# First attention rebuilt by tiles: a three-stage block on one Trainium2 core

## The chip, the cores and the metric

One kernel, launched once, on one core of a Trainium2 chip. Its time is the device time of an execution in microseconds; a time is given as the median of several executions. The core has TensorE (matmuls, weight loads), VectorE, ScalarE, GpSimd, and SyncE, whose queue issues every DMA here. Everything is float32 to the outside.

## The reference

Three blocks follow one another, for 4 images (B) of 576 positions (S). The second block's output is the third's input.

```python
# 1: attention, 8 heads of 64, causal window of 128, distance bias
scores = q @ k.T / 8 + slopes[h] * -abs(rel)      # kept where 0 <= rel < 128
attn = exp(scores - max); attn /= sum + 1e-9
x = (attn @ v)                                    # heads side by side: 512 features
# 2: gated block
h = relu(x @ w_in); u, v = h[:512], h[512:]       # 512 features each
v_n = (v - mean) / sqrt(var + 1e-6)
x = (u * (w_spatial @ v_n + b_spatial)) @ w_out
# 3: four experts of 64 features, top 2 of 4 by x @ w_gate
for e in range(4):
    a = softmax(causal(x @ wq[e] @ (x @ wk[e]).T / 8))
    out += gate[e] * (a @ (x @ wv[e]) @ wo[e])
```

w_in and w_out arrive as 64-bit floats, as integer words, and are turned into float32 on the core.

## The kernel before

**Two kinds of matmul.** Where operands are plain float32, a matmul is two instructions on TensorE. The dense products are done otherwise: an operand is split into a high part (a cast to the reduced form fp32r) and a low part (what is left, `lo_part`, L123), and three products of parts are added up (PASSES, L34). A split costs a cast on ScalarE (or GpSimd) and a subtraction on VectorE for every operand.

**First attention** (L330 to L476, loop L608 to L643). Positions go in five tiles per image, four of 128 and one of 64 (j = 4). The loop has 80 steps (image, tile, pair of heads). Step s does, in this order: `normalise` of step s-1; `scores` of step s (matmuls into one buffer of a PSUM bank, a masked copy that folds the window's two blocks into 128 columns, then for each head a VectorE instruction that adds the bias and takes the row's extreme, and a ScalarE exponential that sums its row: `row_softmax`, L187); some ticks of weight decode; half of the step's dense work; `transposes` of step s-2 (two per step, a ScalarE copy, two GpSimd selects that separate the window's blocks again); the other half; after each tile's fourth step `attend` of the tile three steps back, whose two heads go to two column halves of the array, and whose result is split into x.

For image 0 the score operands are raw float32 on 64 rows, one head at a time. For images 1 to 3 they are split: `load_chunk` (L332) brings K and Q of a tile twice, into both halves of the partitions, and `split_chunk` (L350) makes of K one operand with high part above and low part below (KK), of Q a high and a low copy (qh, ql). Two matmuls of 128 rows then give a head's scores.

**Dense work** is a list of generators (`Dense`, L37) that the loop pulls from by a budget in nominal nanoseconds: 1200 per step up to step 20, then 1650. Per image it holds `v_tile` (5 tiles, 512 columns), `u_half` (2 halves of 4 groups of 12 matmuls, 288 columns) and `spatial` (8 groups of 14). A piece is taken when its x tiles and its weights are there in the order of the program. Each group accumulates in one of three PSUM buffers (psD, L110). `spatial` multiplies by u, splits the result into high and low part and stores both to DRAM (g_dram, L119, L573 to L582).

**Weights.** `in_weights` (L225) decodes w_in in eight pieces on ScalarE, VectorE and GpSimd; the loop advances it by three ticks a step for six steps, then by five (L618). `setup` (L295) prepares the spatial weights, and w_out through DRAM.

**Order.** TensorE's order is that of the program text (L1033). The other engines and SyncE's queue are ordered by a planner at build time, which takes work as it becomes ready by its own estimates.

**Second stage and second attention** (L650 to the end). w_out is folded into the projection weights (`fold`, L678, pw). For each image `load_g` (L702) reads both parts of the gated result; `proj` (L759) makes q, k (pq) and v with gates (pvB). Its `spread` copies the split q and k by DMA into both halves of the partitions, 24 transfers an image, so that `scores_b` (L829) takes two matmuls of 128 rows for each head; tile 4 uses four per half of the columns. PSUM holds three single buffers for scores and two for dense groups (psD). The loop L934 has 40 steps and runs the projection of the next image as dense work.

Of the kernel before, what the change touches and what calls it, by code (L numbers as in the profile page):

```python
# [100 lines left out]
def block_kernel(ctx, tc, qT, qTt, kT, v, w_in, wspT, bsp, w_outT, wcat, wo, rel, relt, low, tri, out):  # L101
# [7 lines left out]
    psX = psA.enter_context(tc.tile_pool(name="psX", bufs=2, space=PSUM))  # L109
    psD = psA.enter_context(tc.tile_pool(name="psD", bufs=3, space=PSUM))  # L110
# [8 lines left out]
    g_dram = dram.tile([B, 2, 4, P, S], F32, name="g_dram")  # L119
# [175 lines left out]
    def setup():  # L295
# [11 lines left out]
        def spatial_bias():  # L307

            st = d2.tile([P, S], F32, tag="f64w", name="st_bias", bufs=2)
            hi = d2.tile([P, S], F32R, tag="g0", name="bias_hi", bufs=2)  # L310
# [19 lines left out]
    raws, QL_, V_ = {}, {}, {}  # L330

    def load_chunk(b, j):  # L332

        q0, qn = TOK[j]
        rq = a1.tile([P, 1024], F32, tag="rawq" if b else "qh", name=f"rq{b}_{j}", bufs=1 if b else 2)
        own = b > 0 or j == 2
        rk = a1.tile([P, H, P], F32, tag="rawk" if own else "ql", name=f"rk{b}_{j}", bufs=1 if own else 2)
        for half in range(2 if b else 1):
            sl = slice(64 * half, 64 * half + 64)
            if j < 4:  # L340
                nc.sync.dma_start(rq[sl, :].rearrange("p (h c) -> p h c", h=H), qT[b, :, :, q0 : q0 + P])
            else:
                nc.sync.dma_start(rq[sl, :768], qTt[b])
            nc.sync.dma_start(rk[sl, :, :qn], kT[b, :, :, q0 : q0 + qn])
        vt = a1.tile([P, 512], F32, tag="v", name=f"v{b}_{j}", bufs=4)
        nc.sync.dma_start(vt[:qn], v[b, q0 : q0 + qn])
        raws[b, j] = (rq, rk)
        V_[b, j] = vt

    def split_chunk(b, j, part):  # L350
        q0, qn = TOK[j]
        rq, rk = raws[b, j]
        w = 1024 if j < 4 else 768
        kk = KK[:, :, q0 : q0 + qn]
        if part == 0:
            nc.scalar.copy(kk, rk[:, :, :qn])
            qh = a1.tile([P, 1024], F32R, tag="qh", name=f"qh{b}_{j}")
            ql = a1.tile([P, 1024], F32R, tag="ql", name=f"ql{b}_{j}")
# [10 lines left out]
    xready, now = {}, [0]  # L369
    st_ = {}  # L370

    def score_operands(b, j, hp, k0, kn):

        heads = []
        for o in range(2):
# [76 lines left out]
    def attend(i):  # L452
# [6 lines left out]
        for t, w in ((j - 1, pT[0]), (j, pT[1])):  # L459
            if t < 0:  # L460
                continue
# [575 lines left out]
```

## Time and profile before

| | us |
|---|---|
| median of 3 runs | 554.91 (551.39 to 555.55) |
| profiled execution | 556.01 |
| its span, first to last instruction | 554.2 |

| engine | busy us | share | instructions |
|---|---|---|---|
| TensorE matmuls | 500.2 | 90% | 3876 |
| TensorE weight loads | 449.2 | 81% | 3876 |
| VectorE | 340.3 | 61% | 1200 |
| ScalarE | 286.8 | 52% | 859 |
| GpSimd | 247.1 | 45% | 536 |

The mean granted TensorE clock was 0.985 of full speed. DMA moved 75.02 MB. The shares are means over stages that differ, so the stretches are to be read one by one. A matmul's duration in the trace holds its passage through the array, which the next one overlaps; how far apart matmuls start says what they cost in a row. In the rows PE is TensorE (PEld its weight loads), DVE VectorE, ACT ScalarE, POOL GpSimd, SP SyncE (SPq its queue), L405 line 405; out<-in names what an instruction writes and reads. An image's tiles are counted on: tile 5 is the first of image 1, tile 10 the first of image 2.

### The profile page before, as it was taken

The page shows a single profiled execution, that of the slowest core. Times are in us where ns is not written, and L with a number is a line of the kernel's source. Part 1 is how long each engine was busy: PE and PEld are TensorE (multiplying, and loading weights), DVE is VectorE, ACT ScalarE, POOL GpSimd, SP SyncE. Part 2 cuts the span into 40 slices and gives each one's busy share as a digit, 9 for nine tenths or more (in the row PEclk, how much of TensorE's full clock was granted, in tenths as well). Part 3 has the DMA queues.
Part 4 walks back from the last instruction along what each step waited for, and adds up shares of the span by engine and source line. Part 5 has one row for each costly group of instructions (what it writes and reads, how often), then busy time and mean ns, then how long its engine had stood idle before and what let it go on. Part 6 is the DMA issues. An engine that isn't in the chain of part 4 may idle for free.

```text
span 554.2 us, 11535 instructions
## 1 busy us (share of the span) xinstructions
PE 500.2 (90%) x3876; PEld 449.2 (81%) x3876; DVE 340.3 (61%) x1200; ACT 286.8 (52%) x859; POOL 247.1 (45%) x536
## 2 busy tenths in 40 slices
PE   4556986898999999999999999989899999999993
PEld 3444776697878899899898999979889999998882
DVE  2899868597877787687654643315463463446640
ACT  4455545475556675566543522324564554565851
POOL 3887864666774688556651000003241232232430
PEclk9999999798999999999999999999999999999997
DMA  9962246645876348621037068289755522641111
GB/s 232 262 195 78 71 117 152 169 118 157 228 188 133 80 93 186 181 73 39 2 130 256 19 238 285 56 209 257 173 190 136 139 60 71 142 117 46 39 39 58
DMA packets 68674, 75.02 MB, mean 135 GB/s; under 512 B 13638, under 2 KB 44486, under 8 KB 68616
## 3 DMA queue, kind: packets, MB, share of 16 engines
q1 hardware_dynamic: 68616, 74.29, 50.0%
q8 instruction: 31, 0.51, 0.4%
q14 instruction: 27, 0.22, 0.1%
HBM read 43.86 MB, written 16.25 MB: 108 GB/s over the span
## 4 chain that ended last, share of the span: by engine, by line
PE 67%; DMA 9%; DVE 9%; POOL 4%; ACT 4%; SPq 3%; issue 2%; DVEq 0%; POOLq 0%; ACTq 0%
PE pv L486 9%; PE pg L566 7%; PE pq L787 7%; PE pvB L808 5%; PE pxB L898 5%; PE pout L916 5%; PE pu L549 5%; DMA rk<-in_kT 5%; PE px L466 4%; PE ps L405 4%; PE psB L840 4%; PE ptB L878 4%; PE pw L686 3%; PE pt L431 2%; PE psB L849 2%
## 5 line engine op out<-in xcount | busy, mean ns | idle before, releaser
L189 ACT ACTIVATE p<-p,st 128x128 f32<-128x128 f32 x144 | 56.8, 396 | 34.0 <-DVE st L188 29.2
L196 POOL TENSOR_SCALAR p<-p,st 128x128 f32<-128x128 f32 x144 | 64.4, 457 | 15.5 <-DVE st L193 12.1
L486 PE MATMUL pv<-win,x 128*128 128x512 f32 x240 | 68.5, 420 | 0.5 <-ACT x L127 0.4
L566 PE MATMUL pg<-wsp,vn 128*128 128x288 f32 x384 | 63.4, 304 | 0.0
L549 PE MATMUL pu<-x,win 128*128 128x288 f32 x384 | 60.2, 301 | 0.0
L192 POOL TENSOR_SCALAR stB<-stB 128x2 f32<-128x2 f32 (+1 forms) x40 | 9.2, 230 | 112.7 <-ACT pB L189 107.2
L787 PE MATMUL pq<-x,W 128*128 128x288 f32 x384 | 56.4, 299 | 0.0
L566 PEld LDWEIGHTS pg<-wsp,vn 128*128 128x128 f32 x384 | 54.5, 192 | 0.0
L549 PEld LDWEIGHTS pu<-x,win 128*128 128x128 f32 x384 | 52.9, 188 | 0.5 <-issue 0.2
L787 PEld LDWEIGHTS pq<-x,W 128*128 128x128 f32 x384 | 52.1, 188 | 0.5 <-DVE hl L124 0.2
L486 PEld LDWEIGHTS pv<-win,x 128*128 128x128 f32 x240 | 44.0, 199 | 8.2 <-ACT x L127 0.9
L196 POOL TENSOR_SCALAR pB<-pB,stB 128x128 f32<-128x128 f32 (+4 forms) x72 | 39.4, 559 | 24.5 <-DVE stB L861 18.9
L189 ACT ACTIVATE pB<-pB,stB 128x128 f32<-128x128 f32 (+3 forms) x64 | 35.8, 560 | 26.8 <-DVE stB L188 24.0
L431 PE MATMUL pt<-ident,p 128*128 128x128 f32 x128 | 30.2, 308 | 18.5 <-POOL p L196 16.3
L192 POOL TENSOR_SCALAR st<-st 128x2 f32<-128x2 f32 (+1 forms) x80 | 25.7, 322 | 40.5 <-ACT p L189 36.0
L444 POOL TENSOR_SCALAR_AFFINE_SELECT pU<-pT 128x256 f32<-128x256 f32 (+1 forms) x64 | 31.6, 494 | 24.8 <-ACT pT L432 12.9
L405 PE MATMUL ps<-rk,rq 64*128 64x128 f32 (+1 forms) x144 | 29.5, 361 | 13.9 <-DMA rk<-in_kT 7.3
L431 PEld LDWEIGHTS pt<-ident,p 128*128 128x128 f32 x128 | 17.8, 147 | 28.1 <-POOL p L196 22.3
L405 PEld LDWEIGHTS ps<-rk,rq 64*128 64x128 f32 x144 | 24.8, 255 | 19.1 <-issue 7.8
L188 DVE CUSTOM_DVE_ANT_0 p<-ps,relm 128x128 f32<-128x128 f32 x128 | 31.5, 283 | 13.3 <-DMA relm<-in_rel 8.7
L188 DVE CUSTOM_DVE_ANT_0 pB<-psB,trit 128x128 f32<-128x128 f32 (+3 forms) x64 | 29.6, 487 | 13.4 <-PE psB L840 13.4
L808 PE MATMUL pvB<-W,x 128*128 128x260 f32 (+1 forms) x240 | 32.8, 286 | 4.3 <-DVE hl L124 4.3
(139 smaller groups left out, 1175.2 us busy)
## 6 DMA issues: line engine op xcount, KB each, us to landing
g_dram<-g SPq DMA_DIRECT2D x32, 288.0 KB, 3.0
q<-hl SPq DMA_DIRECT2D x64, 144.0 KB, 2.8
x<-g_dram SPq DMA_DIRECT2D x8, 1024.0 KB, 5.6
rq<-in_qT SPq DMA_DIRECT2D x28, 256.0 KB, 4.3
rk<-in_kT SPq DMA_DIRECT2D x28, 256.0 KB, 4.6
kk<-hl SPq DMA_DIRECT2D x32, 144.0 KB, 2.5
out<-ot SPq DMA_DIRECT2D x18, 256.0 KB, 2.0
v<-in_v SPq DMA_DIRECT2D x16, 256.0 KB, 3.1
```

Source lines behind the costliest of these rows:

```text
L188: nc.vector.tensor_tensor_reduce(s_view, ps_view, tab, -0.125, FLT_MAX, ALU.add, ALU.min, nm)
L189: nc.scalar.activation(s_view, s_view, AF.Exp, bias=nm, scale=-1.0, accum_out=sm)
L192: nc.gpsimd.tensor_scalar(dst, src, 1e-9, 0.0, op0=ALU.add, op1=ALU.add)
L196: nc.gpsimd.tensor_scalar(p, p, r, 0.0, op0=ALU.mult, op1=ALU.add)
L405: nc.tensor.matmul(ps[:, o, c : c + w], lhs, rhs, start=(n == 0), stop=(n == len(ops) - 1))
L431: nc.tensor.transpose(pt[:, o, :], p[:, o, :], ident)
L444: nc.gpsimd.affine_select(out=u_, in_=h, pattern=[[-i, n] for i, n in pattern], compare_op=ALU.is_gt, fill=0.0, base=0, channel_multiplier=1)
L486: nc.tensor.matmul(pv, x[i][:, k, t0 : t0 + P], win[j][:, k, 512:1024], start=(n == 0), stop=(n == 11))
L549: nc.tensor.matmul(pu[:, :HALF], win[i][:, k, m * P : (m + 1) * P], x[j][:, k, c], start=(n == 0), stop=(n == 11))
L566: nc.tensor.matmul(pg[:, :HALF], vn[i][k][:, m * P : (m + 1) * P], wsp[j][:, k, c], start=(n == 0), stop=False)
L787: nc.tensor.matmul(pq[:, :HALF], W[i][:, k, c0 : c0 + P], G[j][:, k, c], start=(n == 0), stop=(n == 11))
L808: nc.tensor.matmul(pv[:tn, :260], G[i][:, k, COL[t] : COL[t] + tn], W[j][:, k, 512:772], start=(n == 0), stop=(n == 11))
```

## The change

First attention goes by tiles, not by pairs of heads. Q and K come from the host in pairs of heads, one head on partitions 0 to 63 and the other on 64 to 127 (for tile 4 zero-padded, so that one matmul serves both), once each, K whole per image from image 1 on. Nothing of them is split: every image's scores are plain float32, the two heads of a pair on the two row halves of the array and into two banks. Softmax takes groups of four heads; normalisation is one GpSimd multiply with a broadcast operand. One turn of the loop does `attend` of tile s-2, all scores of tile s, the split of x, loads for tile s+2, and then transposes of tile s-1 and softmax of tile s by groups, with six pulls of a sixth of 8200 nominal nanoseconds between. Decode advances by 12 ticks three times a turn in the first six turns. In PSUM scores take two buffers of two banks, dense groups two, attention output one.

The gated result is stored to DRAM once, unsplit; `load_g` reads it into a staging buffer, and casts and subtractions split it there, for images 2 and 3 one part a step. In the second attention q and k are split into their own tiles with no copies; scores use the row halves with three passes; tile 4 uses a zero-padded copy of q made on GpSimd. Scores have one buffer of two banks, dense groups three.

```diff
-    psX = ... bufs=2    psD = ... bufs=3          # first stage
+    psX = ... bufs=1    psD = ... bufs=2
...
+    def load_chunk(b, j):
+        Q_[b, j] = a1.tile([P, 4, P], F32, tag="q", bufs=3)
+        nc.sync.dma_start(Q_[b, j], qP[b, :, j])
+        if j == 0:
+            K_[b] = a1.tile([P, 4, S], F32, tag="k", name=f"k{b}")
+        if b == 0:
+            nc.sync.dma_start(K_[b][:, :, q0 : q0 + qn], kP[b, :, :, q0 : q0 + qn])
+        elif j == 0:
+            nc.sync.dma_start(K_[b], kP[b])
...
+    def scores(b, j):
+        for g in range(2):
+            ps = psS.tile([P, 2, 512], F32, tag="S", name=f"ps{b}_{j}_{g}")
+            for h in range(2):
+                hp = 2 * g + h
+                if j < 4:
+                    for o in range(2):
+                        r = slice(64 * o, 64 * o + 64)
+                        nc.tensor.matmul(ps[:, o, 256 * h : 256 * h + kn], Q_[b, j][r, hp, :], K_[b][r, hp, k0 : k0 + kn], start=True, stop=True)
+                else:
+                    nc.tensor.matmul(ps[:, h, :kn], Q_[b, j][:, hp, :], K_[b][:, hp, k0 : k0 + kn], start=True, stop=True)
+    def softmax(b, j, g):
...
+            nc.vector.copy_predicated(view[:, :, 0:P], lowm..., view[:, :, P:256])
+            for i in range(4):
+                row_softmax(p[:, 2 * h + o, :], view[:, i, 0:P], ...)
+        inverse(sm, sm)
+        nc.gpsimd.tensor_tensor(p[:, :n, :], p[:, :n, :], sm.unsqueeze(2).to_broadcast([P, n, P]), op=ALU.mult)
+    def transposes(b, j, g):
+        for i in range(n):
+            nc.tensor.transpose(pt[:, i, :], p[:, i, :], ident)
+        nc.scalar.copy(here[:, :n], pt[:, :n])
...
     def spatial(b):
-                nc.vector.tensor_mul(g, u[m][:, c], pg[:, :HALF])
-                dense.post.append(lambda ...: nc.scalar.copy(g2[0][:, c], g))
-                dense.post.append(low)
+                nc.vector.tensor_mul(g[:, c], u[m][:, c], pg[:, :HALF])
+                if s == 1:
+                    nc.sync.dma_start(g_dram[b, m], g)
...
+    RATE = 8200.0
+    for s in range(len(tiles) + 2):
+        if s >= 2:
+            px = attend(*tiles[s - 2])
+        if s < len(tiles):
+            scores(*tiles[s])
+        if s >= 2:
+            take(*tiles[s - 2], px)
+        if s + 2 < len(tiles):
+            load_chunk(*tiles[s + 2])
+        dense.pull(RATE / 6)
+        parts(s)                                   # decode and setup ticks
+        for g in range(2):
+            if 1 <= s <= len(tiles):
+                transposes(*tiles[s - 1], g)
+            dense.pull(RATE / 6)
+            if s < len(tiles):
+                softmax(*tiles[s], g)
+            dense.pull(RATE / 6)
+            parts(s)
+        dense.pull(RATE / 6)
...
+    def load_g(b, pool):
+        f = pool.tile([P, 4, S], F32, tag="gf", name=f"gf{b}", bufs=1)
+        nc.sync.dma_start(f[:, :, 64:576], src[:, :, 0:512])
+        nc.sync.dma_start(f[:, :, 0:64], src[:, :, 512:576])
+        def parts():
+            for k in range(4):
+                nc.scalar.copy(G[0][:, k, :S], f[:, k, :])
+                yield
+                lo_part(G[1][:, k, :S], f[:, k, :], G[0][:, k, :S])
+                yield
...
-    psS = ... bufs=3    psD = ... bufs=2           # second attention
+    psS = ... bufs=1    psD = ... bufs=3
     def proj(b, G):
-        def spread(f, pr, role): ...               # copies of q and k by DMA
+        QT[b] = [wk.tile([P, 2, P], F32R, tag=f"qt{i}", name=f"qt{b}_{i}") for i in range(2)]
     def scores_b(i):
-                    nc.tensor.matmul(ps[o][:, :kn], Q[z][:, 2 * pr + o, 128 + q0 : 256 + q0], K[:, 2 * pr + o, 64 : 64 + kn], start=(z == 0), stop=(z == 1))
+            for n, (y, z) in enumerate(PASSES):
+                for o in range(2):
+                    r = slice(64 * o, 64 * o + 64)
+                    nc.tensor.matmul(ps[o][:, :kn], Q[y][r, pr, 64 + q0 : 192 + q0], K[z][r, pr, 64 : 64 + kn], start=(n == 0), stop=(n == 2))
...
+                for n, (y, z) in enumerate(PASSES):
+                    nc.tensor.matmul(ps[s][:, :HALF], QT[b][y][:, pr, :], K[z][:, pr, c], start=(n == 0), stop=(n == 2))
```

## Rows read from the trace of the kernel before

**Rows 1.** By stretch: PE, PEld, DVE, ACT, POOL busy (instructions), clock, DMA share, GB/s

```profile
0.00:55.70 55.70, 31.20 (x114) 22.94 (x115) 42.28 (x108) 26.38 (x73) 38.70 (x59) 1.00 0.73 191
55.70:78.40 22.70, 22.25 (x161) 17.91 (x161) 16.10 (x56) 11.73 (x40) 17.42 (x36) 1.00 0.40 102
78.40:185.20 106.80, 93.21 (x717) 81.78 (x716) 85.42 (x296) 63.12 (x207) 66.07 (x140) 0.95 0.63 156
185.20:334.80 149.60, 148.24 (x1187) 137.54 (x1187) 100.19 (x331) 80.81 (x253) 72.60 (x174) 1.00 0.42 121
...
397.80:554.20 156.40, 146.66 (x1286) 131.40 (x1284) 73.83 (x327) 83.28 (x227) 43.72 (x103) 0.98 0.34 93
```

**Rows 2.** TensorE by line: xcount | busy us, mean ns | idle us before, releasers

```profile
L486 PE MATMUL pv<-win,x 128*128 128x512 f32 x240 | 68.5, 420 | 0.5 <-ACT x L127 0.4
L566 PE MATMUL pg<-wsp,vn 128*128 128x288 f32 x384 | 63.4, 304 | 0.0
L549 PE MATMUL pu<-x,win 128*128 128x288 f32 x384 | 60.2, 301 | 0.0
L787 PE MATMUL pq<-x,W 128*128 128x288 f32 x384 | 56.4, 299 | 0.0
...
L405 PE MATMUL ps<-KK,qh 128*128 128x256 f32 (+2 forms) x120 | 32.0, 289 | 0.1
...
L466 PE MATMUL px<-pT,v 128*64 128x128 f32 (+1 forms) x320 | 30.2, 283 | 0.0
...
L405 PE MATMUL ps<-rk,rq 64*128 64x128 f32 (+1 forms) x144 | 29.5, 361 | 13.9 <-DMA rk<-in_kT 7.3 <-DVE st L188 5.6 <-DVE f L247 0.9
...
L840 PE MATMUL psB<-kk,q 128*128 128x128 f32 (+3 forms) x128 | 26.9, 332 | 0.0
...
L849 PE MATMUL psB<-kk,q 128*128 128x288 f32 (+1 forms) x64 | 10.5, 306 | 0.0
...
L405 PEld LDWEIGHTS ps<-rk,rq 64*128 64x128 f32 x144 | 24.8, 255 | 19.1 <-issue 7.8 <-DVE st L188 6.8 <-DVE f L247 1.2
```

**Rows 3.** Chain of waits that ended last: start us, us, what

```profile
61.80 1.08 PE ps L405 x8
...
220.91 1.90 PE px L466 x32
...
295.39 6.58 PE pv L486 x28
301.97 6.32 PE pu L549 x48
...
364.09 2.78 DMA q<-hl
```

**Rows 4.** VectorE, ScalarE and GpSimd by line and shape, columns as before

```profile
L188 DVE CUSTOM_DVE_ANT_0 p<-ps,relm 128x128 f32<-128x128 f32 x128 | 31.5, 283 | 13.3 <-DMA relm<-in_rel 8.7 <-PE ps L405 4.3
...
L124 DVE TENSOR_TENSOR KK<-rk,KK 64x512 fp32r<-64x512 f32 x24 | 17.1, 750 | 2.0 <-ACT KK L356 1.6
...
L124 DVE TENSOR_TENSOR g<-g,g 128x288 fp32r<-128x288 f32 x32 | 15.6, 487 | 9.2 <-ACT g L581 7.3 <-DMA g_dram<-g 1.8
...
L189 ACT ACTIVATE p<-p,st 128x128 f32<-128x128 f32 x144 | 56.8, 396 | 34.0 <-DVE st L188 29.2 <-POOL pT L446 2.6 <-POOL p L196 0.9
L189 ACT ACTIVATION_READ_ACCUMULATOR p<-p,st 128x1 f32 x144 | 27.1, 188 | 0.0
...
L267 POOL TENSOR_TENSOR u<-u,f 128x512 f32<-128x512 f32 x8 | 11.8, 1472 | 3.0 <-DVE st L193 1.6 <-DVE f L263 1.3
```

**Rows 5.** TensorE's matmuls in order of time, from 208 us

```profile
208.00 0.78 PE L566 MATMUL pg<-wsp,vn 128*128 128x288 f32 x4
208.71 0.44 PE L466 MATMUL px<-pU,v 128*64 128x128 f32 x4
208.98 0.39 PE L466 MATMUL px<-pT,v 128*64 128x128 f32 x4
209.19 0.39 PE L466 MATMUL px<-pU,v 128*64 128x128 f32 x4
```

More of the change, by code (lines that the diff above doesn't have):

```diff
@@ L328, in setup @@
                 yield from out_weights(k, c)
-    raws, QL_, V_ = {}, {}, {}
+    Q_, K_, V_ = {}, {}, {}
     def load_chunk(b, j):
         q0, qn = TOK[j]
[L335 to L348, printed above, removed]
@@ L450, in block_kernel @@
[L450 to L476 removed]
+                nc.vector.copy_predicated(view[:, :, 0:P], lowm[:, 0:P].unsqueeze(1).to_broadcast([P, 4, P]), view[:, :, P:256])
@@ L478, in block_kernel, with take @@
+    def take(b, j, px):
+        q0, qn = TOK[j]
+        if j < 4:
+            split(x[0][:, :, q0 : q0 + P], x[1][:, :, q0 : q0 + P], px)
+        else:
+            twice = [t[:, :, 512:640].rearrange("p m (r c) -> p m r c", r=2) for t in x]
+            split(*twice, px[:, :, :64].unsqueeze(2).to_broadcast([P, 4, 2, 64]))
+        xready[b, j] = now[0]
     stats_, vr = {}, {}
@@ L558, in spatial @@
         for m in range(4):
-            g2 = [d2.tile([P, S], F32R, tag=f"g{i}", name=f"g{b}_{m}_{i}", bufs=2) for i in range(2)]
+            g = d2.tile([P, S], F32, tag="g", name=f"g{b}_{m}", bufs=2)
             for s in range(2):
@@ new lines, in parts @@
+    def parts(s):
+        for _ in range(12 if s < 6 else 8):
+            next(decode, None)
+        for _ in range(2 if 4 <= s < 7 else 3 if s >= 9 else 0):
+            next(prep, None)
+    RATE = 8200.0
+    px = None
+    for s in range(len(tiles) + 2):
+        now[0] = 4 * s
+        if s >= 2:
+            b, j = tiles[s - 2]
+            if j in (0, 2) and b > 0:
+                dense.through(f"u{b - 1}_{j // 2}")
+            px = attend(b, j)
+        if s < len(tiles):
[4 more added lines that the diff above has]
+            load_chunk(*tiles[s + 2])
+        now[0] += 1
+        dense.pull(RATE / 6)
[6 more added lines that the diff above has]
+                softmax(*tiles[s], g)
+            now[0] += 1
+            dense.pull(RATE / 6)
+            parts(s)
+        dense.pull(RATE / 6)
@@ L661, in block_kernel @@
         nc.gpsimd.memset(tie[:, 0, e, 0:e], 1.0)
+    gfp = ctx.enter_context(tc.tile_pool(name="gfp", bufs=1, side="right", reuse_waits="tile"))
     fp_stack = ExitStack()
@@ L833, in scores_b @@
         Q, K = QS[b], KS[b]
-        ps = [psS.tile([P, 512], F32, tag="S", name=f"psB{b}_{j}_{pr}_{o}") for o in range(2)]
+        two = psS.tile([P, 2, 512], F32, tag="S", name=f"psB{b}_{j}_{pr}")
+        ps = [two[:, o, :] for o in range(2)]
         p = wk.tile([P, 2, S], F32, tag="p", name=f"pB{b}_{j}_{pr}", bufs=4)
```

274 lines of the change are left out of this document (84 added, 190 removed).

## The prediction

> **What bounds the kernel now.** I read the busy times by stretch first [rows 1]; the stretches end where the attention output of tile 1, the first u matmul, the attention output of tile 10 and the weight fold begin. From 185.2 to 334.8 us TensorE is busy for 148.24 of 149.60 us: nothing is to be had there but shorter TensorE work. In the first 55.7 us it is busy for 31.20 us while VectorE has 42.28, and from 78.4 to 185.2 for 93.21 of 106.80 with VectorE at 85.42. Busy time of TensorE counts the tail of every isolated matmul, so I counted work instead: instructions [rows 2] times their spacing in unbroken stretches of the chain of waits [rows 3]. v: 240 x 0.235 = 56.4 us; u 384 and spatial 384 (and 64 more at L571, by the code) x 0.132 = 110; attention output 576 (the row shows the 320 that read pT; 256 more read pU) x 0.059 = 34; transposes 144, by the code, at twice that = 17; scores of image 0, 144 x 0.135 = 19; scores of images 1 to 3, 240 (120 with qh, as many with ql) of 128 to 256 columns, put at 0.118, a little under the 0.132 of 288 columns, = 28. That is 264 us in the 334.8 us before the fold, so TensorE stands still for about 70 us. Where: the 275 instructions before 78.4 us [rows 1], half of them image 0's scores, are some 34 us of work, which leaves 44 us idle; I put 3 to 4 us after 185.2; some 22 us remain between 78.4 and 185.2. So the path is VectorE (decoding weights, splitting operands, softmax) up to about 185 us, and TensorE from there to the end, apart from the entry to the second attention, where the chain goes through a copy of hl by DMA [rows 3].
>
> **Start, up to the first u matmul (78.4 us).** VectorE was busy for 42.28 + 16.10 = 58.4 us up to there, and could begin at 8.7 us, when the bias table landed (its wait, [rows 4]); that stays. The new loop advances the weight decode by 36 ticks in its first tile, against 12 for the four steps of the old one, so all eight pieces are ahead of tile 2's softmax in program order. Some 0 to 8 of the 58 us, I estimate, are work that u does not need (spatial and output weights, image 1's splits). VectorE kept full would be ready at 8.7 + 50 to 58 = 59 to 67 us; I take 64: **-14 us**. Bounds: -19 (59) and 0, if TensorE, whose order is fixed, waits for the decode at tile 2 with the transposes of tile 1 behind it. The cheaper image 0 scores (19 us now, below 9 then) count nothing here: VectorE hides them.
>
> **From there to 185 us (22 us idle).** Gone from VectorE: 48 x 0.750 (K's 24 low parts shown, Q's 24 are alike) + 32 x 0.487 (gated result) = 51 us [rows 4], with the K and g casts on ScalarE, the Q conversion on GpSimd and the second copy of every K and Q load. VectorE, 80% busy in this stretch, falls to about 65% at the same rate of tiles. What I expect to stay: about 2 us of changes between array shapes, the chains of the output weights through their single buffers, and gaps around tiles 5 and 10, when no dense work is ready. I leave 10 us: **-12 us** (bounds -18 and -5). On GpSimd one broadcast multiply of 128x512 replaces four scalings; the nearest row is an addition of that size, 1.472 us [rows 4], bounds 0.7 (half) and 1.9 (a third more); two per tile of some 12 us, and the transposes that need it come most of a tile later: nothing. The selects and copies twice as wide and half as many: nothing, by the same cover. If it goes, the attention output of tile s-2 waits for GpSimd at the head of its turn.
>
> **Scores on row halves.** Each float32 matmul is two instructions. The trace has no pair of row halves. It has column halves: four instructions, that is two matmuls of 128 columns, start every 0.22 us [rows 5]; one matmul of 64 rows takes two of 0.135 [rows 3], more than twice as much for each. So a pair of 256 columns is 0.44 us side by side and 0.87 one after the other. Per image: 4 pairs x 0.22, 12 x 0.44, and 8 full-array instructions of 192 columns at 1.5 x 0.11 = 7.4, and 1 us for ten changes of array shape at about 0.1 (four spatial matmuls from 208.00 end at 208.53 by their spacing, the next block starts at 208.71 [rows 5], so 0.18 at most): 8.4 us. Before it was 80 x 0.118 = 9.4. Three images: -3, and image 0's last tile -1: **-4 us**. One after the other: 14.7, so +16 for the three images and +1: +17 us. I take side by side, because column halves are the nearest row.
>
> **Two banks for the dense groups instead of three.** A group of 12 u or spatial matmuls lasts 12 x 0.132 = 1.58 us, and its bank must be emptied within the next one. The second attention runs so already: its projection pq, with two banks, shows no idle time before its matmuls [rows 2]. **+3 us** for some late ones (bounds 0 and the third rival).
>
> **Entry to the second attention.** Scores read the projected q and k in place; the copies (one landing of 2.78 us stands in the chain [rows 3], after its issues by SyncE, and a like one some 24 us later) go. They leave TensorE idle, by my count, about 3 us before the first pvB and 2 us at the second: **-5 us** (bounds -7, -2). New there: four casts and four subtractions per image to split the stored result. Image 0's lie beside the spatial matmuls and the fold, the others beside the last stretch, where TensorE is busy for 146.66 of 156.40 us and VectorE for 73.83: nothing. SyncE loses 96 issues, and the stored result halves.
>
> **Second attention.** 128 instructions [rows 2], 32 each of 128, 256, 384 and 512 columns, at 0.11, 0.12, 0.18 and 0.235: 20.6 us. Three passes of pairs instead of two passes of singles is three quarters: 15.5, and about 4.8 for array changes: 0. The tail has 48 instead of 64 matmuls of 288 columns: **-2 us**. One after the other: six for four, +10, with the changes +15. One scores buffer of two banks instead of three of one: a step lasts some 4 us (156.40 us for about 37 steps) and VectorE reads within 2 us: nothing; if VectorE is late, the next scores wait.
>
> **Sum.** -14 - 12 - 4 + 3 - 5 - 2 = -34. The profiled execution took 556.01 us (span 554.2 and 1.8 around it), 1.1 above the median of the runs; against that median the forecast is **521 us**, by its own bounds 506 to 538.
>
> **Rival 1: the halves take turns.** Two row halves write the same partitions, if different banks; if they don't overlap, +21 in the first stage against the sum and +15 in the second: 521 + 36 = 557 us, no change; half an overlap gives 539. For it: no row shows the pair. Against: the column halves, and that loads of 64 rows x 128 columns take 255 ns on average [rows 2] while matmuls of the very same 64 rows follow each other every 0.135 us: loads are hidden though the rows are the same. The Trainium skill (TensorE: Matmul & The Clock Gate, Part 3: Packing small matmuls, The mechanism) says that a weight load overlaps running matmuls only where their row groups differ; by that rule each half would add its loads to its matmuls and the time would come near this rival's, but this trace's loads contradict it. Chance 0.15.
>
> **Rival 2: the start does not move.** TensorE sits at the first v, waiting for decoded weights, and DMA (73% of the first stretch) brings them no sooner, since the larger early loads of K and V queue ahead. Then the -14 is lost: 535 us. For it: the DMA share. Against: VectorE was the busier. Chance 0.15.
>
> **Rival 3, slower: ScalarE is late at the two banks.** Softmax now comes as four exponentials in a row, 4 x (0.396 + 0.188) = 2.34 us [rows 4]. An evacuation of about 0.4 us behind them comes 2.7 us after its group, with the next one over after 1.58: TensorE waits 1.15. It decides from half of the 64 groups of u and spatial on (37 us, the gain is gone); with two of three caught, 49 us, it is 570 us. The Trainium skill (TensorEngine Tiling (Array Packing), PSUM Bottleneck) warns that faster TensorE work leaves the evacuation as the limit; no row here shows it. Against: ScalarE is busy for only 63.12 of 106.80 us [rows 1], and it sheds casts. Chance 0.10.
>
> **How the numbers follow.** Forecast 0.55, rivals 0.15, 0.15, 0.10, and 0.05 for better than 506. A change under 1% (549.4 to 560.5) can't be told from none. Faster: 0.55 + 0.14 + a quarter of rival 1 + 0.03 = 0.76; same 0.09; slower 0.15 (rival 3 and the worse end of rival 1). The range 502 to 556 leaves out rival 3, the upper part of rival 1 and a little below.
>
> **What would show it.** Start: first u matmul near 64 us. Middle: attention output of tile 10 near 165, with VectorE under 70%. Scores: pairs starting together, a tile's 16 instructions in about 1.9 us; 3.5 means rival 1. Two banks: idle time before u and spatial matmuls put down to ScalarE or VectorE means rival 3. Entry: pvB right behind pq. Wrong altogether if TensorE idles at the head of tiles for the selects on GpSimd.

## The result, and the profile after

The changed kernel takes 558.8 us (median of 10 runs, 555.9 to 560.8 for nine of them) where the kernel before takes 555.2 beside it: ratio 1.0065, 95% interval 1.0035 to 1.0094. The tenth run took 939.8 us at a granted clock of 1.0 and is left out of the ratio. The forecast of 521 us and its range, 502 to 556, are both missed, on the side of the slower kernel. The profiled execution took 560.76 us, its span 559.0; it is the longest of the nine, so a stretch read from it can be some us long.

| | before | after |
|---|---|---|
| span, us | 554.2 | 559.0 |
| TensorE matmuls busy, us | 500.2 | 487.7 |
| VectorE, ScalarE, GpSimd busy, us | 340.3, 286.8, 247.1 | 296.4, 265.4, 176.7 |
| DMA, MB | 75.02 | 44.34 |
| mean granted clock | 0.985 | 0.939 |

Every engine does less and the span is longer. (The clock of the kernel before is put too high in its first 59 us, see run 8.) The kernel after by stretch, with the columns and the first four stretches of [rows 1], then to the second attention's first steps, then to the end:

```profile
0.00:55.70 55.70, 22.52 (x112) 15.55 (x112) 43.36 (x104) 26.59 (x77) 30.12 (x37) 0.77 0.63 207
55.70:78.40 22.70, 14.70 (x85) 11.49 (x86) 17.93 (x49) 9.54 (x29) 11.05 (x14) 0.65 0.32 100
78.40:185.20 106.80, 97.69 (x748) 85.59 (x747) 60.19 (x233) 53.84 (x183) 36.06 (x62) 0.94 0.32 104
185.20:334.80 149.60, 148.44 (x1171) 135.39 (x1171) 71.75 (x248) 66.82 (x203) 40.67 (x78) 0.99 0.24 81
334.80:397.80 63.00, 62.23 (x470) 58.53 (x469) 31.11 (x106) 29.90 (x81) 12.89 (x39) 1.00 0.13 39
397.80:559.00 161.20, 142.08 (x1250) 119.89 (x1248) 72.03 (x315) 78.72 (x218) 45.89 (x116) 0.97 0.09 31
```

Fixed stretches hide what moved, so I read the same events in both traces and took differences:

| stretch | before | after | change | forecast |
|---|---|---|---|---|
| up to the first u matmul | 78.4 | 82.2 | +3.8 | -14 |
| to the attention output of tile 10 | 106.8 | 106.5 | -0.3 | -12 |
| to the fold | 149.7 | 140.4 | -9.3 | -1 (scores -4, dense banks +3) |
| to the second attention's first attention output | 62.3 | 59.7 | -2.6 | -5 |
| from there to the end | 157.0 | 170.2 | +13.2 | -2 |

One trace of a stretch is good to about 4 us: runs 1 and 2 below have the kernel after's order of work until just before the fold, and their folds begin at 326.4 and 325.1 us, not at 329.1.

Two places hold the loss: the start, 18 us worse than forecast, and the second attention, 15 us worse. The middle is better than its row says: between the first u matmul and tile 10 the kernel after ran 192 u and 84 v matmuls against 144 and 76, so 48 x 0.132 + 8 x 0.235 = 8.2 us of the work that the old kernel does in the third stretch [spacings of rows 3] had been done there. Less idle time was worth about 8 us, scores and banks together about -1, as forecast.

**The second attention.** TensorE's waits in the kernel after from 360 us (us in total, times, longest), where the kernel before has none at its scores:

```profile
PE psB L802 <- DVE stB L803: 7.8, 8, 2.3
PE psB L795 <- DVE stB L188: 1.1, 1, 1.1
...
```

The weight loads of the same matmuls, which come first, stand longer:

```profile
PEld psB L802 <- DVE stB L803: 9.7, 8, 2.6
```

One of the waits in order of time, on TensorE and on VectorE (start, us, what; in brackets the idle time before):

```profile
401.31 0.64 PE L802 MATMUL psB<-k,qt 128*128 128x288 f32 x3
403.30 0.66 PE L802 MATMUL psB<-k,qt 128*128 128x288 f32 x3 [1.35 <-DVE stB L803]
```

```profile
401.55 0.63 DVE L705 TENSOR_TENSOR c<-c,c 128x80 f32<-128x80 f32 x1
...
402.38 0.41 DVE L832 COPY pTB<-ptB 128x256 f32<-128x256 f32 x1
...
402.78 0.45 DVE L803 CUSTOM_DVE_ANT_0 pB<-psB,tritail 128x288 f32<-128x288 f32 x1
```

In tile 4 the two halves of the columns go to the two banks of one buffer. The program puts VectorE's reading of the first half between them, so the second half waits until VectorE, busy with gates and a copy, has read the first. The second half goes to another bank and needs nothing of the first: it waits because the two banks are one buffer of the program. It is so in all eight tails.

**The start.** TensorE's waits in the kernel after from 8 to 90 us:

```profile
PE pt L397 <- ACT pT L398: 13.9, 3, 6.9
PE px L422 <- POOL pU L405: 9.4, 3, 6.0
PE ps L361 <- DMA k<-in_kP: 7.0, 1, 7.0
PE px L422 <- POOL pT L406: 2.1, 1, 2.1
PE pv L443 <- ACT win L275: 1.8, 1, 1.8
...
```

Tile 1's turn in order of time, TensorE and then ScalarE:

```profile
36.99 2.51 PE L443 MATMUL pv<-win,x 128*128 128x512 f32 x5 [1.75 <-ACT win L275]
39.30 1.06 PE L397 MATMUL pt<-ident,p 128*128 128x128 f32 x4
...
43.12 0.66 PE L397 MATMUL pt<-ident,p 128*128 128x128 f32 x4 [1.63 <-ACT pT L398]
49.80 0.70 PE L422 MATMUL px<-pU,v 128*64 128x128 f32 x4 [6.02 <-POOL pU L405]
```

```profile
42.49 0.58 ACT L398 COPY pT<-pt 128x512 f32<-128x512 f32 x1
46.88 0.40 ACT L189 ACTIVATE p<-p,st 128x128 f32<-128x128 f32 x1 [3.81 <-DVE st L188]
...
49.43 0.57 ACT L398 COPY pT<-pt 128x512 f32<-128x512 f32 x1
```

GpSimd in the same turn:

```profile
46.04 1.72 POOL L267 TENSOR_TENSOR u<-u,f 128x512 f32<-128x512 f32 x1 [1.29 <-DVE f L263]
47.83 0.74 POOL L311 MEMSET st_bias<- 32x576 f32 x1
48.64 1.11 POOL L405 TENSOR_SCALAR_AFFINE_SELECT pU<-pT 128x512 f32<-128x512 f32 x1
```

The first v group stands ahead of tile 1's transposes and waits for decoded weights. The second group of transposes then waits for the one transposes bank; its own copy, possible from 43.8 us, starts at 49.43, since in ScalarE's order the next tile's exponentials come first and wait for VectorE. The first group's copy was done at 43.07, but its select on GpSimd stands behind decode work and starts at 48.64. One late engine passes its delay to the next.

VectorE was not what the first u matmul came last for. Its last piece of w_in, in the kernel after and in the kernel before:

```profile
65.12 0.69 DVE L124 TENSOR_TENSOR win<-u,win 128x512 fp32r<-128x512 f32 x1
```

```profile
63.59 0.69 DVE L124 TENSOR_TENSOR win<-u,win 128x512 fp32r<-128x512 f32 x1
```

The weights were decoded at 65.8 us (64.3 before), and the first u matmul began at 82.2 (78.4). In between, in the kernel after, stand tile 2's transposes (they wait 5.3 us for the bank, until 70.4), its attention output from 73.0, the split of its x, which ends at 78.4, and a v group.

**80 to 110 us.** The chain that ended last runs through stores of the output weights:

```profile
80.96 7.28 DMA wt_dram<-hi_wout
...
88.26 0.43 ACT r_wout L147
88.68 0.31 ACT u L510
...
89.03 1.85 PE pu L506 x12
...
95.35 3.03 DMA wt_dram<-lo_wout
...
105.89 2.71 DMA wt_dram<-lo_wout
```

A chain's first instruction on ScalarE waits for the buffer that the chain before is still storing, and the evacuation of u stands behind it.

**Row halves run side by side.** A tile's 16 score instructions, in the chain after:

```profile
140.69 1.93 PE ps L361 x16
```

The forecast said 1.9, and 3.5 for halves that take turns: the first rival is out. The two halves' instructions start 7 ns apart there, and the next pair follows 0.22 us later, with weight loads of 0.19 us each running beside the matmuls of both halves. The Trainium skill (TensorE: Matmul & The Clock Gate, Part 3: Packing small matmuls) lets loads overlap running matmuls where row groups differ; between the halves they do, and the row agrees. That the halves' loads would add up by this rule was my misreading.

### The profile page after: what moved, and what is told of

It reads as the page before. It is cut to its first block, busy times and chain, and to the rows that moved or that the text cites. A ratio compares the mean times of both kernels' runs of the same rounds, so it can differ in the third digit from the quotient of the medians.

```text
span 559.0 us, 10572 instructions
## 1 busy us (share of the span) xinstructions
PE 487.7 (87%) x3828; PEld 426.4 (76%) x3828; DVE 296.4 (53%) x1052; ACT 265.4 (47%) x788; POOL 176.7 (32%) x345
## 2 busy tenths in 40 slices
DMA packets 26588, 44.34 MB, mean 79 GB/s; under 512 B 5926, under 2 KB 10150, under 8 KB 26152
## 4 chain that ended last, share of the span: by engine, by line
PE 68%; DVE 12%; DMA 6%; ACT 4%; POOL 3%; issue 3%; SPq 2%; DVEq 0%; POOLq 0%; ACTq 0%
PE pq L736 9%; PE pv L443 8%; PE pu L506 7%; PE pg L523 7%; PE px L422 6%; PE pvB L760 5%; PE pout L869 4%; PE pxB L851 4%; PE psB L795 3%; PE ptB L831 3%; PE pw L635 3%; PE ps L361 3%; PE pt L397 2%; ACT p L189 2%; DMA v<-in_v 2%
## 5 line engine op out<-in xcount | busy, mean ns | idle before, releaser
L506 PE MATMUL pu<-x,win 128*128 128x288 f32 x384 | 57.3, 305 | 5.1 <-ACT vr L451 3.6
L523 PE MATMUL pg<-wsp,vn 128*128 128x288 f32 x384 | 59.1, 299 | 0.0
L192 POOL TENSOR_SCALAR st<-st 128x4 f32<-128x4 f32 (+1 forms) x40 | 10.7, 266 | 118.1 <-ACT p L189 116.5
L361 PE MATMUL ps<-k,q 64*128 64x256 f32 (+1 forms) x256 | 36.0, 431 | 13.0 <-DMA k<-in_kP 13.0
L387 POOL TENSOR_TENSOR p<-p,st 128x512 f32<-128x512 f32 (+1 forms) x40 | 39.7, 991 | 12.5 <-DVE st L193 11.8
L361 PEld LDWEIGHTS ps<-k,q 64*128 64x128 f32 x256 | 26.7, 230 | 18.6 <-issue 7.8
L397 PE MATMUL pt<-ident,p 128*128 128x128 f32 x144 | 24.8, 294 | 15.6 <-ACT pT L398 15.6
L422 PE MATMUL px<-pT,v 128*64 128x128 f32 (+1 forms) x320 | 32.1, 295 | 5.3 <-POOL pT L406 4.2
L422 PE MATMUL px<-pU,v 128*64 128x128 f32 (+1 forms) x256 | 27.0, 293 | 9.5 <-POOL pU L405 9.4
L188 DVE CUSTOM_DVE_ANT_0 p<-ps,relm 128x128 f32<-128x128 f32 x128 | 29.5, 286 | 8.4 <-DMA relm<-in_rel 7.7
```

The source lines that it names most:

```text
L188: nc.vector.tensor_tensor_reduce(s_view, ps_view, tab, -0.125, FLT_MAX, ALU.add, ALU.min, nm)
L361: nc.tensor.matmul(ps[:, o, 256 * h : 256 * h + kn], Q_[b, j][r, hp, :], K_[b][r, hp, k0 : k0 + kn], start=True, stop=True)
L387: nc.gpsimd.tensor_tensor(p[:, :n, :], p[:, :n, :], sm.unsqueeze(2).to_broadcast([P, n, P]), op=ALU.mult)
L397: nc.tensor.transpose(pt[:, i, :], p[:, i, :], ident)
L422: nc.tensor.matmul(px[64 * o : 64 * o + 64, hp, :qn], V_[b, t][:kb, h * 64 : h * 64 + 64], rhs, start=(t == max(0, j - 1)), stop=(t == j))
L506: nc.tensor.matmul(pu[:, :HALF], win[i][:, k, m * P : (m + 1) * P], x[j][:, k, c], start=(n == 0), stop=(n == 11))
```

## The experiments

Runs are numbered as below. All ratios are to the kernel before on the same chip, with 95% intervals; the changed kernel's is 1.0065. Times of events (first u, tile 5, fold) are starts in the run's trace.

### The second attention: one buffer of two banks

**1. Two single buffers.**

```diff
-        two = psS.tile([P, 2, 512], F32, tag="S")
-        ps = [two[:, o, :] for o in range(2)]
+        ps = [psS.tile([P, 512], F32, tag=f"S{o}") for o in range(2)]
```

> The changed kernel, with the two banks of second-attention scores as two single buffers, each with its own name, in place of one buffer of two banks; PSUM use is the same. Theory (one buffer holds up the next scores): in the changed kernel the second half of tile 4's scores waits for VectorE's reading of the first half, 7.8 us in 8 places, and the first matmul of a step waits for both heads' softmax. Then the tails take about 1 us instead of 1.6 to 3.6, and the time falls by 6 to 10 us, to about 550. Rival (the pairs themselves, three passes and changes of array shape, cost it): no change, within 2 us, and the waits show up at the next matmul.

Measured 0.9813 (0.9778 to 0.9848), 546.3 us: 2.5% below the changed kernel, more than the theory said. Up to the second attention the orders of all engines are the changed kernel's. From fold to end it takes 218.2 us against 229.9, and of TensorE's waits from 360 us one is left:

```profile
PE ptB L830 <- ACT pTB L831: 0.4, 1, 0.4
```

**2. The second attention of before in the changed kernel** (`proj`, `scores_b` and PSUM of before; the unsplit result stays).

> The changed kernel with the projection, the scores and the PSUM buffers of the second attention as they were before the change (copies of q and k by DMA, two matmuls of 128 rows a head, three single score buffers, two dense ones); the first stage and the unsplit stored result stay new. Theory (the second attention loses what the first stage won): from the fold on it needs about 219 us as before, against 230, so about 548 to 550 us. Rival (the loss comes from the unsplit result, its casts and subtractions): the last images stay slow, 556 to 560 us.

Measured 0.9943 (0.9918 to 0.9967), 552.6 us. Fold to end 223.8 us: 66.9 to the first attention output (62.3 before), 156.9 from there (157.0 before). The time lies between the two ranges. So the loop's loss is not in the unsplit result; but at the entry, where the projection's first groups now wait for VectorE to empty the two dense banks, splitting it costs about 4.6 us:

```profile
PE pq L746 <- DVE hl L124: 4.0, 3, 2.4
```

In run 1, with three dense banks and without the copies, the entry takes 59.7 and the loop 158.5.

**3. The reverse: the kernel before with one buffer of two banks, and three dense ones.**

> The kernel before with one edit, the reverse of an earlier one: the second attention's scores get one buffer of two banks instead of three of one, and the dense groups three instead of two, as in the changed kernel. Its copies, its two matmuls of 128 rows a head and its first stage stay. Theory (the one buffer alone slows the second attention): waits before the second half of tile 4's scores appear, 6 to 9 us in 8 places, and the time rises by 8 to 14 us, ratio 1.015 to 1.025. Rival (it costs only together with the pairs' three passes): ratio 0.995 to 1.005.

Measured 1.0073 (1.0042 to 1.0104), 560.5 us: between the two ranges. The three dense banks help the entry (58.5 us instead of 62.3, with the copies by DMA still there), which the theory had left out; the loop went from 157.0 to 165.3 us, with the changed kernel's waits at tile 4:

```profile
PE psB L850 <- DVE stB L851: 5.1, 8, 1.0
PE psB L841 <- DVE stB L188: 1.1, 2, 1.0
...
```

The buffer is shown as the cause in both directions, and this run has no row halves.

### The start: order, transposes bank, weights

**4. v behind the transposes.** `now[0] > xready[b, t] + (2 if b == 0 else 0)` in the readiness of v and u.

> The changed kernel, with the v products of image 0 ready two quarters of a turn later in the order of the program, so that they stand behind the transposes of the next tile and not ahead of them. Theory (the first v products wait for decoded weights, and tile 1's transposes, 4 to 9 us late, wait behind them in TensorE's fixed order): tile 1's transposes at about 35 us instead of 39 to 44, its attention output complete about 5 us earlier, the first u matmul at 75 to 78 instead of 82 us, the time 3 to 6 us lower. Rival (VectorE, full from 20 to 60 us, sets the start whatever TensorE's order is): first u still at 80 to 84 us and no change of the time.

Measured 0.9889 (0.9859 to 0.9919), 550.2 us. First u 74.9 us, fold 321.7 (329.1): more than expected. But 3.2 us of the gain lie in the second attention, whose code is untouched (167.0 us from the first attention output instead of 170.2): with the planner's other order the waits at tile 4 are shorter,

```profile
PE psB L802 <- DVE stB L803: 5.9, 8, 1.0
```

From 8 to 90 us TensorE's wait for the copies out of the transposes bank is now the largest, 20.5 us in 3 places.

**5. The output weights later.** A one-element copy from x of tile 5 into the load's buffer, so that the load waits; the preparation also begins later in the order of the program.

> The changed kernel, with the preparation of the output weights held back: its first load waits until the attention output of tile 5 is cast. Theory (this work, which u and the spatial products do not need, was drawn forward into the start, and its chain through the DRAM stores holds ScalarE between 80 and 110 us): VectorE sheds some 4 us before the first u matmul and ScalarE's waits for the stores (5.1 us in 4 places) go; first u at 78 to 80, attention output of tile 5 some 5 to 10 us earlier than 114, the time 5 to 10 us lower. Rival (the softmax and the selects of tiles 1 and 2 set the start, and the chain runs beside them): no change, within 2 us.

Measured 1.0006 (0.9972 to 1.0041): 0.6% below the changed kernel, hardly clear of noise. First u 78.7 and tile 5 at 111.6 us (125.0), as the theory had it, but the fold only at 328.2: the gain was given back.

**6. Both edits (1 and 4).**

> The changed kernel with both earlier edits: the v products of image 0 behind the transposes, and two single score buffers in the second attention. Theory (the two losses lie in different stretches and add): against the kernel before 0.9813 of the second edit times 0.9889/1.0065 of the first, 0.964, so about 537 us where before takes 557. Rival (the earlier start is given back in the first stage): 0.975 to 0.981.

Measured 0.9709 (0.9655 to 0.9763), 542.7 us: between the two. The edits overlap by the 3.2 us that run 4 had won in the second attention, which takes 158.5 us here as in run 1; the fold, at 323.7, is within a trace's scatter of run 4's.

**7. Both, and all weights later** (spatial weights behind tile 2, output weights behind tile 5; from turn 5 on three ticks of preparation at a time).

> Both edits, and the spatial weights' loads wait for the attention output of tile 2, the output weights' for that of tile 5, so that neither is worked on by VectorE and ScalarE in the start. Theory (VectorE, 37 of 40 us busy from 20 to 60 us, sets the start): it sheds the 7.7 us of low parts of the spatial weights there, first u matmul at 66 to 70 us instead of 75, the time 3 to 6 us below both edits alone. Rival (transposes that wait for ScalarE's copy out of the one transposes bank, 20.5 us in 3 places, set the start): first u at 73 to 76 and no gain, or a loss of up to 4 us from weights that are late at the spatial products.

Measured 0.9670 (0.9615 to 0.9724): not told apart from run 6. First u 73.8: the rival's.

**8. Both, and dummy matmuls** in the first turns.

```diff
+    for _ in range(n):
+        nc.tensor.matmul(pd, relm[:, 0, 0, :], relm[:, 0, 0:4, :], start=True, stop=True)
```

> Both edits, and 104 matmuls of 128 columns by 512 in bf16 on constants, whose result nobody reads, between the scores and transposes of the first turns of the loop; nothing else changes. Theory (the granted clock, 0.65 to 0.76 from 20 to 60 us where the kernel before had 1.00, costs time): the clock there rises to 0.9 or more, scores of a tile take 1.7 instead of 3 us, first u at 70 to 73 instead of 75, the time 2 to 4 us lower. Rival (TensorE mostly waits there, and the waits are on other engines): the clock rises and the time does not fall, or rises by the dummies' own 1 to 4 us.

Measured 0.9785 (0.9719 to 0.9851), first u 84.0 us: slower than run 6, but in another order of the engines from 27 us on, so the clock can't be priced by it. The theory took the clock from the column of [rows 1], which is no guide here. It gives 0.65 for 20 to 40 us in run 4 and 0.96 in run 6, yet a tile's 16 score instructions run at the lower level (1.2 GHz) in both; with the dummies they run at the higher (2.4 GHz). Runs 4, 6 and 8:

```profile
30.55 3.11 PE L361 MATMUL ps<-k,q 64*128 64x256 f32 x16
```

```profile
31.76 3.63 PE L361 MATMUL ps<-k,q 64*128 64x256 f32 x16
```

```profile
37.77 2.00 PE L361 MATMUL ps<-k,q 64*128 64x256 f32 x16
```

And it gives 1.00 up to 78.4 us of the kernel before, where eight like instructions take 2.07 us and then 1.16:

```profile
48.58 2.07 PE L405 MATMUL ps<-rk,rq 64*128 64x128 f32 x8
...
59.30 1.16 PE L405 MATMUL ps<-rk,rq 64*128 64x128 f32 x8
```

So the kernel before was at the lower level there, too. Close to the first u the clock does cost the kernel after something: from 73 to 77 us (0.50) the attention output of tile 2 starts its groups of four matmuls every 0.43 us, in run 4 at 2.4 GHz every 0.22, some 1.7 us over eight groups.

**9. Both, and a second bank for transposes.**

```diff
-        pt = psT.tile([P, 4, P], F32, tag="T", ...)
+        pt = (psX if g else psT).tile([P, 4, P], F32, tag="X" if g else "T", ...)
```

> Both edits, and the transposes of a tile's second group of heads go to the bank of the attention output, which is free between the split of one tile and the attention output of the next. Theory (the one transposes bank, emptied by ScalarE only behind exponentials that wait for VectorE, holds TensorE in the start: 20.5 us in 3 places): these waits fall below 8 us, first u at 68 to 72 us instead of 75, the time 3 to 6 us below both edits alone. Rival (the copies themselves are late, and the selects and the attention output wait for them anyway): the wait moves to the attention output behind the selects, first u within 2 us, no change.

Measured 0.9558 (0.9509 to 0.9607), 534.4 us; the gain over run 6 is larger than expected. First u only 1 us earlier (74.2), but tile 5 at 96.9 us (105.2) and the fold at 313.9 (323.7). Both theories erred on where: in the waits of TensorE from 8 to 75 us those for the bank are gone, and attention output waits for the copies instead,

```profile
PE px L422 <- ACT pT L398: 8.8, 1, 8.8
```

while the turns behind it have become shorter.

**10. The second bank alone in the changed kernel.**

> The changed kernel with one edit: the transposes of a tile's second group of heads go to the bank of the attention output. The v products stay ahead of the transposes and the second attention keeps its one score buffer. Theory (the one transposes bank is the larger part of what the start lost): fold at 316 to 322 us instead of 329, the time 7 to 12 us lower, 0.985 to 0.993 of before. Rival (the bank counts only once the v products are out of the way): fold at 326 to 329, no change.

Measured 0.9905 (0.9875 to 0.9936), 551.0 us: a gain in the theory's range by ratio, but not where the theory had it. First u comes at 79.5 us (82.2), but the fold, at 324.6, is hardly earlier than in run 2 with the old bank (325.1), and 3.5 us of the gain lie in the second attention (166.7 us instead of 170.2), whose code is untouched.

**11. Run 9, all weights later.**

> Both edits, the second transposes bank, and the weights held back as before (spatial weights behind tile 2, output weights behind tile 5). Theory (with the transposes free, VectorE, 19.94 of 20 us busy from 40 to 60 us, sets the start, so shedding the 7.7 us of the spatial weights' low parts tells now): first u at 66 to 70 us instead of 74, the time 3 to 7 us below the version without, 0.943 to 0.951 of before. Rival (GpSimd and the order of ScalarE set it, or the weights come late at the spatial products): first u at 72 to 75, the ratio 0.953 to 0.960.

Measured 0.9616 (0.9585 to 0.9648). First u at 69.6 us, as the theory said, and the time just above the rival's range. Between 180 and 200 us the held-back output weights stand between softmax and gated product on VectorE, and TensorE waits with both dense banks full:

```profile
190.81 1.33 PE L527 MATMUL pg<-wsp,vn 128*128 128x288 f32 x8 [2.82 <-DVE g L533]
```

**12. Run 9, K of image 1 later.**

> Both edits and the second transposes bank, and the whole K of image 1 (1.18 MB, issued at 19 us ahead of five pieces of w_in) is loaded only once the attention output of tile 1 is cast. Theory (the start is not held by DMA, the raw buffers of w_in are freed by VectorE): first u within 1.5 us of 74 and the time within 2 us. Rival (the larger early loads of K queue ahead of w_in, as the second rival of the prediction had it): the fourth to sixth pieces land 3 us earlier, first u at 70 to 72, the time 2 to 4 us lower.

Measured 0.9718 (0.9680 to 0.9756), 540.5 us, first u 78.8: both theories fail. A piece of w_in landed at 26.8 us instead of 29.3, yet the fourth piece's low part came at 42.6 instead of 36.1, because the planner, given one other load, ordered VectorE otherwise from 30 us on. Weights that land earlier are not enough, then; what DMA would be worth in an unchanged order is not shown. And 1.6%, the loss against run 9, is what a small edit with its reordering can do here.

**13. Run 9, only the spatial weights later.**

> Both edits, the second transposes bank, and of the weights only the spatial ones held back (behind the attention output of tile 2); the output weights are free again. Theory (VectorE set the start, and holding the output weights gave the gain back, between 180 and 200 us, by VectorE's late reading of the two dense banks): first u at 69 to 72 us, no stall of 4 to 5 us between tiles 11 and 12, fold at 309 to 312 instead of 314, ratio 0.945 to 0.953. Rival (an earlier start is worth nothing here, since the dense work is short of VectorE later whatever is held): first u at 69 to 72, ratio 0.955 to 0.962.

Measured 0.9741 (0.9710 to 0.9772): slower than run 9 with a first u at 68.3 us. Neither theory. Waits of ScalarE, then of VectorE, from 100 to 180 us:

```profile
ACT r_wout L147 <- DMA wt_dram<-hi_wout: 10.1, 4, 3.2
...
```

```profile
DVE f_wout L149 <- DMA wt_dram<-lo_wout: 8.4, 3, 5.1
...
```

**14, 15, 16. Two buffers for the output weights' chains**, in run 13, in run 9 and alone in the changed kernel; the decode of w_in has two f tiles instead of three, to make room.

```diff
-            r = pool.tile([P, 256], F32, tag="f64r", bufs=1)       # f64f, hi and lo alike
+            r = pool.tile([P, 256], F32, tag="f64r", bufs=2)
```

> The kernel of the last run (both edits, second transposes bank, spatial weights behind tile 2), with two buffers instead of one for each of the two work tiles of the output weights' chains, so that a chain does not wait for the store of the one before; w_in's decode has two f tiles instead of three to make room. Theory (the last run gave its start of 68 us back because ScalarE and VectorE, in order, stood before the next chain's first instructions until the stores to DRAM had landed: 10.1 us in 4 places on ScalarE and 8.4 in 3 on VectorE from 100 to 180 us): these waits fall below 4 us, the matmuls' waits for vr and u (6.2 and 4.4 us) with them, fold at 308 to 314 us instead of 322, ratio 0.945 to 0.958. Rival (any change of the planner's order moves the middle by some us, the stores only show the wait): fold at 318 to 324, ratio 0.968 to 0.976.

> Both edits and the second transposes bank, with two buffers instead of one for the work tiles of the output weights' chains (and two f tiles in w_in's decode). Theory (the stores hold ScalarE here for only 2.6 us in one place from 100 to 180 us): a gain of 0 to 4 us, ratio 0.949 to 0.957. Rival (two f tiles slow the decode): first u 1 to 3 us later than 74, ratio 0.957 to 0.963.

> The changed kernel with this one edit alone: two buffers for the work tiles of the output weights' chains (and two f tiles in w_in's decode). Theory (between 80 and 110 us the stores hold ScalarE 5.1 us in 4 places, and u's matmuls behind it): u's waits go, attention output of tile 5 at 117 to 121 us instead of 125, the time 3 to 8 us lower, ratio 0.992 to 1.001. Rival (the transposes bank sets the pace there as well): tile 5 at 123 to 126, no change.

Measured 0.9531 (0.9490 to 0.9572) for run 14, 533.6 us, first u 67.7 and fold 312.3: the waits for stores are gone from ScalarE and VectorE, and with them 2.1% against run 13. Run 15: 0.9594 (0.9546 to 0.9641), no gain over run 9, first u 76.0, as its rival said. Run 16: 0.9869 (0.9811 to 0.9927), 552.6 us, 2.0% better than the changed kernel, tile 5 at 116.9 instead of 125.0 us: more than its theory said. Runs 9 and 14 take 4.4 and 4.7% less than the kernel before; their intervals overlap.

## Why the prediction was wrong

**Second attention, -2 forecast, +13.2 measured: the step "one scores buffer of two banks instead of three of one ... nothing".** It compared a whole step (4 us) with VectorE's reading (2 us, for which it names no row) and left out that tile 4 writes both banks within one step with a reading between. Runs 1 and 3 put the price at 11.7 us in the new kernel and 8.3 in the old. With two buffers the pairs take 158.5 us from the first attention output against 157.0, so the forecast saving of 2 us isn't there either: about +1.5. The Trainium skill (TensorEngine Tiling (Array Packing), Gotcha 1: PSUM Pressure) says that row tiling raises the pressure on PSUM, since row tiles write to different banks. The pairs here do write to two banks; but the 7.8 us are not the row tiles' own, since tile 4's matmuls use the whole array (128*128 in their rows) and run 3 has such waits with no row halves: the cost is that of the one buffer. I had weighed the neighbouring section on evacuation against ScalarE in the first stage, and not where one buffer took the place of three.

**Start, -14 forecast, +3.8 measured: the step from "VectorE kept full would be ready" to the first u matmul.** The readiness itself came out: VectorE was full, 37.3 of 40 us from 20 to 60 (17.39 + 19.94), and had the weights decoded at 65.8 us, within the 59 to 67 named. But it had them at 64.3 in the kernel before as well, so this readiness was not what held the first u; that came 16.4 us after it (14.1 before), since x of tile 2 has to be there too. That path goes through ScalarE's in-order copies, the one transposes bank, GpSimd's selects and TensorE's order. Of the full time 7.7 us were low parts of spatial weights, which u doesn't need; the prediction had allowed 0 to 8 for such work. The bound named beside it (0, if TensorE waits for the decode with the transposes of tile 1 behind it) is one of the holds, worth 7.3 us of the first u in run 4; TensorE's own wait for decoded weights is 1.8 us, against 13.9 for the transposes bank and 11.5 for the selects. Run 14, with order, bank, spatial weights and chains mended, has its first u at 67.7 us, 3.7 after the 64 taken: nearly reached, but not by this change.

**Middle, -12 forecast, about -8 in work done.** VectorE fell to 60.19 of 106.80 us, 56% (forecast 65). "The chains of the output weights through their single buffers" stood in the prediction among what stays, within 10 us; in run 16 a second buffer gave 2.0%, some 11 us over the whole kernel, in run 15 it gave nothing, so it has no fixed price.

**Scores -4 and dense banks +3: right.** Together about -1 by subtraction. By the starts in the two traces an image's scores take TensorE 8.2 us (3 x 1.93 + 1.27 + 1.09, forecast 8.4) against 9.6, -4.3 for three images, which leaves about +3 for the banks, within a trace's scatter. Of late dense banks the kernel after shows 5.1 us before u (0.0 in [rows 2]), all in the middle stretch:

```profile
L506 PE MATMUL pu<-x,win 128*128 128x288 f32 x384 | 57.3, 305 | 5.1 <-ACT vr L451 3.6 <-ACT u L510 1.5
...
L387 POOL TENSOR_TENSOR p<-p,st 128x512 f32<-128x512 f32 x32 | 34.8, 1086 | 10.7 <-DVE st L193 10.7
```

The second row is the broadcast multiply, taken at 1.472 us between bounds of 0.7 and 1.9: 1.086.

**Entry, -5 forecast, -2.6 measured: the step "the copies go".** pvB does come right behind pq, at 360.0 us. But run 3 keeps copies and split result, has three dense banks as the changed kernel, and its entry takes 58.5 us, less than the 59.7. So the gain is the third bank's, -3.8 us, which the sum had left out; given that bank, taking the copies away and splitting the stored result here cost 1.2 us together, and which does what is not shown. The conversion was put at nothing; with two dense banks it cost 4.6 (run 2).

**The sum.** The bounds beside its terms add up to 505 to 545 us, not to 506 to 538; the result lies outside both.

**The rivals.** The first is out. The second had the right outcome (the start doesn't move) for the wrong reason: TensorE's wait for decoded weights at v is 1.8 us, and run 12, with a piece of w_in landing 2.5 us earlier, gained nothing. The third named the right kind of thing, results left too long in too few banks, but ScalarE at two dense banks was not the place: it was VectorE at the score buffer, and the transposes.

**What stays open.** The gains don't add: 1.8% for the order, 1.6 for the bank, 2.0 for the chains, each alone against the changed kernel, and every one reorders the other engines. Of the first two, 3.2 and 3.5 us lie in the second attention and go again with the two score buffers. Run 12 shows that a reordering can be worth 1.6%. Which part of each gain is the named wait is not settled; so the causes in the start are argued from the waits, and only the score buffer's is shown by experiment.

## What to carry to other kernels

Count PSUM buffers by what happens between two writes to the same buffer, not by banks: where a reading stands in program order between writes to two banks of one tile, make them two tiles. On in-order engines, ask for each copy that frees a bank what stands before it and what that waits for; a full engine upstream is not the path by itself. An earlier start is worth something only if what fills the stretch behind it isn't waiting on its own stores.

## What was not expected of the hardware

VectorE's simple decode steps depend on GpSimd. In the kernel after the same instruction took 1.48 us while GpSimd ran a subtraction of two tensors (18.80 to 20.34 us), and 0.42 us at 40.90, when GpSimd was idle:

```profile
19.15 1.48 DVE L251 TENSOR_SCALAR u<-f 128x512 int32<-128x512 int32 x1
...
```

```profile
40.90 0.42 DVE L251 TENSOR_SCALAR u<-f 128x512 int32<-128x512 int32 x1
...
```

It is so in all 18 traces here. Of this step and its like (L259, the same shape and type), the 108 that start while GpSimd works on two tensors take 0.64 to 1.50 us, 1.19 in the mean; the 68 that run with GpSimd idle take 0.40 to 0.43. So "VectorE's busy time" in the start is no fixed amount of work: an edit that moves GpSimd's work moves it too. The Trainium skill (GPSIMD Engine Reference, 1. Specifications) says that the two share their interfaces to SBUF, with contention for VectorE instructions in a 2-port mode or with two SBUF inputs. The step has one input, so by that sentence it would run in such a mode, which no view of these traces names; that GpSimd slows it they show.
